# A drain of GpSimd between the row stores of the last two blocks of an attention and mixture-of-experts kernel

## The chip, the cores and the metric

The kernel runs on one NeuronCore of one Trainium2 chip. The metric is the device time of one execution in microseconds (us), taken as the median of several runs. A separate execution is recorded by the hardware profiler; its rows are quoted below.

## The reference

Four batches of 5056 tokens with 256 channels go through an attention over channels, and the result, 20224 rows of 256 values, through a mixture of eight experts of which each token takes the best one:

```python
qn = q / (norm(q, axis=1) + 1e-06); kn = k / (norm(k, axis=1) + 1e-06)
a = softmax(kn.transpose(0, 2, 1) @ qn / tau)
x = (v @ a).reshape(20224, 256)
logits = x @ w_gate + modality_bias[modality_id]
e_idx = argmax(logits); gate_w = softmax(logits)[e_idx]
for e in range(8):
    mask = e_idx == e
    out[mask] = gate_w[mask, None] * (relu(x[mask] @ w1[e]) @ w2[e])
```

## The kernel before, in words

All matrix products are made with numbers split into a high and a low part, three products for one. The kernel walks over 40 groups of 512 tokens. For each group it makes the rows of x, chooses each token's expert, and writes the rows to a place of that expert in a table in DRAM, `xs`. This takes four indirect DMAs of up to 128 rows each, issued by GpSimd (POOL in the profile).

The second half of the work is in blocks. A block is 512 rows of one expert: SyncE (SP) loads its rows and the expert's weights, TensorE (PE) multiplies by `w1` (`m1`, L642), ScalarE (ACT) and VectorE (DVE) apply the rectifier and split the result, PE multiplies by `w2` (`m2`, L658). `finish(t)` then scales a quarter of the block's result into the tile `yo` on ACT (L669), and `scatter` (L401) stores those 128 rows at their tokens' places in `out`, again with an indirect DMA of POOL. The rows on either side of such a DMA are found by a list of 128 indices in SBUF, and GpSimd builds the DMA's descriptors itself. There are 40 blocks in the usual case (`NB_MIN`), so POOL issues 160 such DMAs to `xs` and 160 to `out`.

After the last group only blocks are left. The pieces of a block run in program order; the stores of one block stand among the pieces of the next (`block_stream` puts the `last` pieces of the block before behind the first piece of the new one). The last block (slot 39) has its two halves finished one after the other: two stores, three more groups of products, two stores.

Behind the last block a value is read by all engines, and a branch on it decides whether further blocks are left over. In the usual case none are, the branch leads to the end, and there each engine's queue takes a few bookkeeping steps: POOL waits for the counts of its DMAs, executes one instruction that adjusts the semaphores of its DMAs (INC_SWDGE_SEM, L797), then a drain (L831); SP waits for the counts of all engines and DMAs; then all engines meet at a barrier, POOL clears the semaphores, and they meet again. This tail is not written in the kernel: it is what the framework puts behind every program. Lines of the kernel that the steps touch: `scatter` and its L401, `finish`, the loop `while chosen < NB_MIN or waiting`, and L797 and L831, which stand for the branch and for the program's end.

Of the kernel before, what the change touches and what calls it, by code (L numbers as in the profile page):

```python
# [34 lines left out]
def kernel(  # L35
# [13 lines left out]
    nc = tc.nc  # L49
# [17 lines left out]
    NB_MIN = -(-T // BLK)  # L67
# [81 lines left out]
    def pad_rows(r):  # L149
        ins = nc.sync.dma_start(  # L150
            xs[bass.ds(r, BLK), :].rearrange("(p t) c -> p t c", t=BLK // P),
            pad.unsqueeze(1).to_broadcast([P, BLK // P, XW]),
        )
        pads.append(ins.ins)
        tc.declare_no_dep(
            ins.ins, group="xr", reason="pads go past the last row of an expert, and before the blocks with them"
        )
# [242 lines left out]
    def scatter(dst, idx, rows, groups, add, bound, why):  # L400
        ins = nc.gpsimd.indirect_dma_start(  # L401
            out=dst, out_offset=bass.IndirectOffsetOnAxis(ap=idx, axis=0), in_=rows, in_offset=None,
            bounds_check=bound, oob_is_err=False,
        )
        for group in groups:
            tc.declare_no_dep(ins.ins, group=group, reason=why)
        for group in add:
            tc.add_to_no_dep_group(group, ins.ins)
        return ins.ins
# [130 lines left out]
        )  # L540


    def pick(g, slot, tail):
        nc.vector.tensor_copy(end9[:, 0:E], bases[g][0:1, :])
        sh = [1, E + 1]
        rem = p2.tile(sh, F32, tag="rem", name=f"rem_{slot}")
        nc.vector.tensor_tensor(rem, end9, nxt9, ALU.subtract)
        nc.vector.scalar_tensor_tensor(
            rem, rem, 1.0 if tail else float(BLK), prio9, ALU.is_ge, ALU.mult
        )  # L550
        m = p2.tile([1, 1], F32, tag="pm", name=f"pm_{slot}")
        nc.vector.tensor_reduce(m, rem, AX.X, ALU.max)  # L552
        nc.vector.tensor_scalar(rem, rem, m, None, ALU.is_equal)
        pr = p2.tile([1, 2, E + 1], F32, tag="pr", name=f"pr_{slot}")
        nc.vector.tensor_tensor(pr[:, 0, :], rem, nxt9, ALU.mult)
        nc.vector.tensor_tensor(pr[:, 1, :], rem, eid9, ALU.mult)
        pk = p2.tile([1, 2], F32, tag="pk", name=f"pk_{slot}")
        nc.vector.tensor_reduce(pk, pr, AX.X, ALU.add)
        pki = p4.tile([1, 2], I32, tag="pki", name=f"pki_{slot}")
        nc.vector.tensor_copy(pki, pk)  # L560
        nc.vector.tensor_tensor(rem, rem, inc9, ALU.mult)
        nc.vector.tensor_tensor(nxt9, nxt9, rem, ALU.add)
        return pki
# [5 lines left out]
    def block_pieces(g, slot, pki, tail):  # L569
# [18 lines left out]
        def load_w(hf):  # L588
            if hf == 0:
                st["e"] = nc.sync.value_load(pki[0:1, 1:2], min_val=0, max_val=E - 1)  # L590
            e = st["e"]
            a = p3.tile([P, CH, FH], F32, tag="w1r", name=f"w1r_{slot}_{hf}")
            c = p3.tile([P, JH, D], F32, tag="w2r", name=f"w2r_{slot}_{hf}")
            nc.sync.dma_start(
                a,
                w1[bass.ds(e, 1), :, hf * FH : (hf + 1) * FH].rearrange("o (h p) f -> p (o h) f", p=P),
            )
            nc.sync.dma_start(
                c,
                w2[bass.ds(e, 1), hf * FH : (hf + 1) * FH, :].rearrange("o (j p) c -> p (o j) c", p=P),  # L600
            )
            st["wr"][hf] = (a, c)
# [61 lines left out]
        def finish(t):  # L664
            if t == 0:
                st["yo"] = p2.tile([P, TT, D], F32, tag="yo", name=f"yo_{slot}")
            yo = st["yo"][:, t, :]
            xr = st["xr"].bitcast(F32)
            nc.scalar.activation(  # L669
                yo, st["y"][t // 2][:, t % 2, :], AF.Copy, scale=xr[:, t, D : D + 1]  # L670
            )
            scatter(
                out, st["xr"].bitcast(I32)[:, t, D + 1 : D + 2], yo, ["y"], ["y"], T - 1,
                "each token has a row of its own",
            )

        prep = [lambda: load_w(0), lambda: load_w(1), load_x]
        prep2 = [lambda: split_w(0), lambda: tr_x(0), lambda: tr_x(1), lambda: split_w(1)]
# [2 lines left out]
        for j in range(1, NJ):  # L681
# [5 lines left out]
            else:  # L687
                body.append(lambda j=j: m2(j - 1))
        last = [lambda: m2(NJ - 1)] + [lambda t=t: finish(t) for t in range(TT)]
        if slot == NB_MIN - 1:  # L690

            last = [lambda: m2(NJ - 1, range(0, 2)), lambda: finish(0), lambda: finish(1)]
            last += [lambda j=j: m2(j, range(2, 4)) for j in range(NJ - 3, NJ)]
            last += [lambda: finish(2), lambda: finish(3)]
# [3 lines left out]
    def run(pieces):  # L698
        for f in pieces:
            f()  # L700
# [10 lines left out]
    waiting = []  # L711
# [3 lines left out]
    def once(blk, what):  # L715
        key = (blk["slot"], what)
        if key not in done:
            done.add(key)
            run(blk[what])

    def block_stream(blk, nxt):

        once(blk, "load")
        once(blk, "prep")
        body = list(blk["body"])
        if nxt is not None:
            once(nxt, "load")
            done.add((nxt["slot"], "prep"))
            at = [len(body) * (i + 4) // 8 for i in range(len(nxt["prep"]))]
            for o, f in reversed(list(zip(at, nxt["prep"]))):  # L730
                body.insert(o, f)
        before = open_blk[0]["last"] if open_blk[0] is not None else []
        open_blk[0] = blk
        return [blk["first"]] + before + body
# [3 lines left out]
    for g in range(G):  # L738
        b, s = divmod(g, NS)
        streams = []  # L740
        for gg, blk in waiting:
            if gg <= g - LAG + 1:
                once(blk, "load")
        if len(waiting) > 0 and waiting[0][0] <= g - LAG:
            _, blk = waiting.pop(0)
            streams.append(block_stream(blk, waiting[0][1] if waiting and waiting[0][0] <= g - LAG + 1 else None))
        soft = list(softmax_pieces(b)) if s == 0 and b > 0 else []
        streams.append(soft + (va[g + 1][0] if g + 1 < G else []) + va[g][1])
        if b + 1 < B:
            streams.append(list(kq_pieces(b + 1, s)))  # L750
        _interleave(*streams)
        if waiting and waiting[0][0] <= g - LAG + 1:
            once(waiting[0][1], "load")
            once(waiting[0][1], "prep")
        if s == NS // 2 and b + 1 < B:
            setup_bias(b + 1)
        n = slots_by(g)
        while chosen < n:
            waiting.append((g, block_pieces(g, chosen, pick(g, chosen, False), False)))
            chosen += 1  # L760
# [7 lines left out]
    for e in range(E):  # L768
        r = nc.sync.value_load(endi[0:1, e : e + 1], min_val=0, max_val=E * CAP)
        pad_rows(r)  # L770
    while chosen < NB_MIN or waiting:
        while chosen < NB_MIN and len(waiting) < 2:
            blk = block_pieces(G - 1, chosen, pick(G - 1, chosen, True), True)
            once(blk, "load")
            waiting.append((G, blk))
            chosen += 1
        _, blk = waiting.pop(0)
        run(block_stream(blk, waiting[0][1] if waiting else None))
    run(open_blk[0]["last"])


# [5 lines left out]
    def left_over(slot, n):  # L787
        if n <= 0:
            return
        rem = p1.tile([1, E + 1], F32, tag="lrem", name=f"lrem_{slot}")  # L790
        nc.vector.tensor_tensor(rem, end9, nxt9, ALU.subtract)
        left = p1.tile([1, 1], F32, tag="left", name=f"left_{slot}")
        nc.vector.tensor_reduce(left, rem[:, 0:E], AX.X, ALU.max)
        lefti = p1.tile([1, 1], I32, tag="lefti", name=f"lefti_{slot}")
        nc.vector.tensor_scalar(lefti, left, 0.0, 1.0, ALU.max, ALU.min)
        lv = nc.values_load(lefti[0:1, 0:1], min_val=0, max_val=1)
        with tc.If(lv > 0):  # L797
            for i in range(min(n, 4)):
                blk = block_pieces(G - 1, slot + i, pick(G - 1, slot + i, True), True)
                run(blk["load"] + blk["prep"] + [blk["first"]] + blk["body"] + blk["last"])  # L800
            left_over(slot + 4, n - 4)
# [34 lines left out]
```

## Time and profile before

| what | us |
|---|---|
| median of 3 runs | 1270.14 |
| lowest and highest of them | 1269.83, 1273.26 |
| the profiled execution's own time | 1270.21 |
| its span, first to last instruction | 1268.1 |
| PE busy within the span | 1235.1 (97%) |
| POOL busy within the span | 348.6 (27%) |

The span lacks 2.1 us of the profiled execution's own time. "Busy" on the page counts an engine's work only. Instructions that only wait, set registers, branch or drain are left out of it, and so are the issues of DMAs on the queues. They appear in the view of one source line, under the name of the engine's queue (POOLq, SPq and so on), with the smallest, median and largest duration in ns and the start of the first and the last.

### The profile page before, as it was taken

Reading aid. Unit: us, or ns where it says so; the run is one execution under the profiler, and the core shown is the slowest. Engines: PE = TensorE matmul, PEld = TensorE weight load, DVE = VectorE, ACT = ScalarE, POOL = GpSimd, SP = SyncE. Lnnn points to the kernel's source line nnn. Section 1 sums busy time; section 2 is a strip of 40 time slices with the busy share of each in tenths; the row PEclk is TensorE's granted clock in tenths of the full one; section 3 lists DMA queues with packets and bytes.
Section 4 is the critical chain, followed back from the end, with each engine's and each line's share of the span. In section 5 each row is a group of like instructions: output and inputs, shape, how many; then the busy total and the mean of one; then the engine's idle time right before and its main releaser. Section 6 shows DMA issues by size and latency. Waiting matters only on the chain.

```text
span 1268.1 us, 24269 instructions
## 1 busy us (share of the span) xinstructions
PE 1235.1 (97%) x8368; PEld 1122.6 (89%) x8368; DVE 856.4 (68%) x2330; ACT 753.0 (59%) x1533; POOL 348.6 (27%) x348
## 2 busy tenths in 40 slices
PE   7998999999999999999999999999999999999994
PEld 6897988999999999999999999999999999999994
DVE  7898967867767767777777776565566655755541
ACT  6876756766666666766666665555555554555441
POOL 0036243232222223222232333222223332221121
PEclk9998999999999999999999999999999999999997
DMA  9759854555555555555555544345444444474300
GB/s 314 250 188 296 277 174 156 158 194 167 183 167 165 171 190 169 162 169 167 167 176 182 182 156 141 136 150 168 143 162 140 162 147 134 152 229 168 134 31 15
DMA packets 113124, 215.34 MB, mean 170 GB/s; under 512 B 16224, under 2 KB 61792, under 8 KB 112992
## 3 DMA queue, kind: packets, MB, share of 16 engines
q1 hardware_dynamic: 97632, 172.11, 43.6%
q0 software_dynamic: 15360, 41.60, 8.6%
q8 instruction: 67, 1.10, 0.4%
q14 instruction: 65, 0.53, 0.1%
HBM read 167.33 MB, written 46.60 MB: 169 GB/s over the span
## 4 chain that ended last, share of the span: by engine, by line
PE 80%; issue 3%; DVE 1%; DMA 1%; POOL 1%; ACT 0%; SPq 0%; POOLq 0%; DVEq 0%; ACTq 0%
PE hp L642 32%; PE y L658 32%; PE xp L469 8%; PE g L277 3%; PE vtp L453 2%; PE xtp L624 2%; PE g L281 2%; POOL out_dram L401 1%; DMA k<-in_k_dram 0%; DMA out_dram<-yo,xr 0%; PE ns L323 0%; PE gw L379 0%; DMA modi<-in_moe_modality_id_dram 0%; DVE hl L646 0%; PE atp L369 0%
## 5 line engine op out<-in xcount | busy, mean ns | idle before, releaser
L658 PE MATMUL y<-w2h,hh 128*128 128x256 f32 x1280 | 360.8, 282 | 0.0
L658 PE MATMUL y<-w2l,hh 128*128 128x256 f32 x1280 | 355.6, 278 | 0.0
L658 PE MATMUL y<-w2h,hl 128*128 128x256 f32 x1280 | 355.3, 278 | 0.0
L401 POOL DMA_INDIRECT xs<-x,pi x160 | 175.2, 1095 | 646.2 <-ACT w1h L613 467.5
L646 DVE SCALAR_TENSOR_TENSOR hl<-hp,hh 128x512 fp32r<-128x512 f32 x320 | 219.6, 686 | 132.5 <-ACT hh L645 131.8
L645 ACT ACTIVATE hh<-hp 128x512 fp32r<-128x512 f32 x320 | 191.9, 600 | 182.4 <-PE hp L642 182.3
L642 PE MATMUL hp<-xh,w1h 128*128 128x512 f32 x640 | 259.4, 406 | 0.2 <-ACT xh L629 0.2
L642 PE MATMUL hp<-xl,w1h 128*128 128x512 f32 x640 | 253.4, 396 | 1.2 <-DVE xl L630 1.2
L642 PE MATMUL hp<-xh,w1l 128*128 128x512 f32 x640 | 253.3, 396 | 0.0
L658 PEld LDWEIGHTS y<-w2h,hh 128*128 128x128 f32 x1280 | 240.3, 188 | 12.9 <-ACT hh L645 0.2
L658 PEld LDWEIGHTS y<-w2l,hh 128*128 128x128 f32 x1280 | 241.4, 189 | 11.5
L658 PEld LDWEIGHTS y<-w2h,hl 128*128 128x128 f32 x1280 | 239.5, 187 | 0.1
L401 POOL DMA_INDIRECT out_dram<-yo,xr x160 | 160.6, 1004 | 191.0 <-ACT yo L669 150.4
L614 DVE TENSOR_TENSOR w2l<-w2r,w2h 128x512 fp32r<-128x512 f32 x160 | 110.5, 691 | 70.5 <-ACT w2h L613 70.4
L642 PEld LDWEIGHTS hp<-xh,w1l 128*128 128x128 f32 x640 | 120.6, 189 | 28.7
L613 ACT CAST w2h<-w2r 128x512 fp32r<-128x512 f32 x160 | 100.2, 626 | 74.0 <-PE y L658 67.2
L614 DVE TENSOR_TENSOR w1l<-w1r,w1h 128x512 fp32r<-128x512 f32 x160 | 109.7, 686 | 49.3 <-ACT w1h L613 48.7
L642 PEld LDWEIGHTS hp<-xl,w1h 128*128 128x128 f32 x640 | 120.6, 189 | 16.1 <-DVE xl L630 1.7
L613 ACT CAST w1h<-w1r 128x512 fp32r<-128x512 f32 x160 | 100.9, 630 | 57.1 <-PE hp L642 56.7
L642 PEld LDWEIGHTS hp<-xh,w1h 128*128 128x128 f32 x640 | 120.2, 188 | 14.6 <-ACT xh L629 0.3
L277 PE MATMUL g<-qs,ks 128*128 128x512 f32 (+1 forms) x320 | 122.4, 405 | 6.5 <-DVE qs L252 5.7
L469 PE MATMUL xp<-ah,vh 128*128 128x264 f32 x320 | 96.3, 301 | 5.4 <-DVE pm L552 2.9
(151 smaller groups left out, 1852.0 us busy)
## 6 DMA issues: line engine op xcount, KB each, us to landing
w1r<-in_moe_w_dram SPq DMA_DIRECT2D x80, 512.0 KB, 3.5
w2r<-in_moe_w_dram SPq DMA_DIRECT2D x80, 512.0 KB, 3.5
xr<-xs SPq DMA_DIRECT2D x40, 516.0 KB, 4.8
v<-in_v_dram SPq DMA_DIRECT2D x36, 512.0 KB, 5.5
q<-in_q_dram SPq DMA_DIRECT2D x35, 512.0 KB, 9.2
k<-in_k_dram SPq DMA_DIRECT2D x35, 512.0 KB, 5.7
xs<-pad SPq DMA_DIRECT2D x9, 516.0 KB, 5.5
xs<-x,pi POOLq DMA_INDIRECT x160, 5.1
```

The lines of the kernel that those rows point to most:

```text
L277: nc.tensor.matmul(g, ks[:pp, t, m * P : (m + 1) * P], qs[:pp, t, :], start=first, stop=False, skip_group_check=True,)
L281: nc.tensor.matmul(g[:, 0:C], ks[:pp, t, C + m * P : C + (m + 1) * P], qs[:pp, t, 0:C], start=False, stop=last, skip_group_check=True,)
L401: ins = nc.gpsimd.indirect_dma_start(out=dst, out_offset=bass.IndirectOffsetOnAxis(ap=idx, axis=0), in_=rows, in_offset=None, bounds_check ...
L453: nc.tensor.matmul(tp[:, t * P : (t + 1) * P], st["v"][:, t, h * P : (h + 1) * P], ident, is_transpose=True, start=t == 0, stop=True, skip ...
L469: nc.tensor.matmul(xp[:, 0:DE], a[:, h, t * P : (t + 1) * P], w[:, h, :], start=i == 0, stop=i == len(seq) - 1,)
L613: nc.scalar.copy(hi, src)
L614: nc.vector.tensor_tensor(lo, src, hi.bitcast(F32), ALU.subtract)
L624: nc.tensor.matmul(tp[:, t * P : (t + 1) * P], st["xr"][:, t, h * P : (h + 1) * P], identr, is_transpose=True, start=t == 0, stop=True, sk ...
L642: nc.tensor.matmul(hp, w[:, h, fs], x[:, h, :], start=i == 0, stop=i == len(seq) - 1)
L645: nc.scalar.activation(hh, hp, AF.Relu)
L646: nc.vector.scalar_tensor_tensor(hl, hp, 0.0, hh.bitcast(F32), ALU.max, ALU.subtract)
L658: nc.tensor.matmul(y, a[:, tsl], w[:, j % 2, :], start=(j == 0 and i == 0 and t % 2 == 0), stop=(j == NJ - 1 and i == 2), skip_group_check ...
```

## The change

A drain instruction is put on POOL's queue behind the four stores of the last block but one (slot 38) and ahead of the four stores of the last block (slot 39). `stored` collects the former, `order` ties them to the drain and the drain to the latter; the ties are for the order on the one queue alone and carry no semaphore (`NoSync`). The drain is put into the last block's list of pieces four pieces before its end.

```diff
+    stored = []
+    drained = []
...
-            scatter(
+            ins = scatter(
                 out, st["xr"].bitcast(I32)[:, t, D + 1 : D + 2], yo, ["y"], ["y"], T - 1,
                 "each token has a row of its own",
             )
+            if slot == NB_MIN - 2:
+                stored.append(ins)
+            elif slot == NB_MIN - 1:
+                order(ins, drained)
...
+    def order(ins, others):
+        for other in others:
+            tc.add_manual_dep(
+                ins, other.name,
+                mybir.DependencyInfo(mybir.DependencyClass.NoSync, mybir.DependencyReason.DATA),
+                reason="order on the stores' queue",
+            )
+
+    def retire():
+        ins = nc.gpsimd.drain()
+        order(ins.ins, stored)
+        drained.append(ins.ins)
...
-        run(block_stream(blk, waiting[0][1] if waiting else None))
+        pieces = block_stream(blk, waiting[0][1] if waiting else None)
+        if not waiting:
+
+            pieces.insert(len(pieces) - 4, retire)
+        run(pieces)
```

In the built program this is one instruction more, on POOL's queue, between the fourth store of slot 38 and the first of slot 39. It waits for no semaphore and sets none. Every other instruction of every engine keeps its place and its waits.

## Rows read from the trace of the kernel before

**Rows 1.** The page: the span, and the busy time of PE and POOL.

```profile
span 1268.1 us, 24269 instructions
PE 1235.1 (97%) x8368; PEld 1122.6 (89%) x8368; DVE 856.4 (68%) x2330; ACT 753.0 (59%) x1533; POOL 348.6 (27%) x348
```

**Rows 2.** Windows over the last 38 us: stretch, length, busy time by engine, clock, DMA.

```profile
core 0: us, PE busy (x) PEld busy (x) DVE busy (x) ACT busy (x) POOL busy (x), PEclk, DMA share, GB/s
1230.00:1250.00 20.00, 20.00 (x132) 18.00 (x131) 5.46 (x8) 5.87 (x12) 3.49 (x5) 1.00 0.07 27
1250.00:1254.80 4.80, 0.72 (x7) 0.52 (x5) 0.00 (x0) 0.91 (x3) 3.87 (x4) 0.96 0.23 75
1254.80:1268.10 13.30, 0.00 (x0) 0.00 (x0) 0.00 (x0) 0.00 (x0) 0.00 (x0) 0.50 0.02 7
```

**Rows 3.** The chain that ended last, its end: start, length, what.

```profile
1249.98 3.44 DMA out_dram<-yo,xr
...
1253.81 0.97 POOL out_dram L401
```

**Rows 4.** POOL's timeline from 1225 us on: start, length, idle before and its end.

```profile
1229.58 0.97 POOL L401 DMA_INDIRECT out_dram<-yo,xr  x1 [18.28 <-ACT yo L669]
...
1233.41 0.97 POOL L401 DMA_INDIRECT out_dram<-yo,xr  x1 [0.31 <-issue]
1249.98 0.97 POOL L401 DMA_INDIRECT out_dram<-yo,xr  x1 [15.60 <-ACT yo L669]
1251.25 0.97 POOL L401 DMA_INDIRECT out_dram<-yo,xr  x1 [0.30 <-ACT yo L669]
1252.53 0.97 POOL L401 DMA_INDIRECT out_dram<-yo,xr  x1 [0.30 <-issue]
1253.81 0.97 POOL L401 DMA_INDIRECT out_dram<-yo,xr  x1 [0.30 <-issue]
```

**Rows 5.** L401 over the whole span, and, from 1229 us on, its DMAs' landing.

```profile
L401 POOL DMA_INDIRECT xs<-x,pi x160: 938/973/2542, 80.1 to 1091.6; - x160
L401 POOL DMA_INDIRECT out_dram<-yo,xr x160: 971/973/1533, 149.7 to 1253.8; - x160
...
DMA to landing us min/median/max: 2.3/2.4/2.4
```

**Rows 6.** The branch behind the last block, L797, on POOL from 1255 us on.

```profile
L797 POOLq EVENT_SEMAPHORE  x2: 43/43/43, 1255.3 to 1256.1; - x2
L797 POOLq INC_SWDGE_SEM  x1: 2306/2306/2306, 1256.2 to 1256.2; - x1
```

**Rows 7.** The program's end, L831, from 1258 to 1262 us: ns min/median/max, starts.

```profile
L831 SPq EVENT_SEMAPHORE  x12: 28/28/28, 1258.5 to 1259.2; - x12
L831 SPq DRAIN  x2: 7/10/13, 1259.2 to 1259.3; - x2
L831 POOLq DRAIN  x1: 8730/8730/8730, 1258.6 to 1258.6; - x1
```

**Rows 8.** L831 from 1262 us on, and the two later drains of POOL.

```profile
L831 POOLq EVENT_SEMAPHORE  x4: 17/17/17, 1267.3 to 1268.0; - x4
...
L831 POOLq EVENT_SEMAPHORE_RANGE_CLEAR  x1: 177/177/177, 1267.7 to 1267.7; - x1
...
L831 POOLq DRAIN  x2: 40/74/107, 1267.5 to 1267.9; - x2
```

**Rows 9.** The program's start, L818: the same two instructions of POOL.

```profile
L818 POOLq INC_SWDGE_SEM  x1: 31/31/31, 0.1 to 0.1; - x1
...
L818 POOLq DRAIN  x1: 188/188/188, 0.3 to 0.3; - x1
...
L818 POOL MEMSET const-uint8-127<- x1: 119/119/119, 0.3 to 0.3; 128x1 uint8 x1
```

**Rows 10.** Drains of the other engines at L831.

```profile
L831 DVEq DRAIN  x2: 10/14/17, 1251.3 to 1267.6; - x2
L831 PEldq DRAIN  x2: 8/8/8, 1252.9 to 1267.6; - x2
L831 ACTq DRAIN  x2: 8/8/8, 1254.2 to 1267.6; - x2
```

## The prediction

> **What bounds the kernel now.** I read the page first. PE is busy for 97% of the span [rows 1], so up to the last product nothing but PE's work sets the time, and an instruction on POOL, busy for 27%, can move the end only where PE has stopped. So the second view is the windows over the last stretch [rows 2]. The reader is to see three stages there. Until 1250.0 PE is busy without a gap. From 1250.0 to 1254.8 POOL issues the last stores. From 1254.8 to 1268.1, 13.3 us, no engine is busy at all, and the DMAs move almost nothing. The third view, the chain of waits, ends at 1253.81 + 0.97 = 1254.8 with the last store [rows 3]: it follows counted work and says nothing about those 13.3 us. They are 1.05% of the span, and they have to be read from the queues' own rows, by source line.
>
> Those rows give the tail step by step. The last store was issued at 1253.8 and lands 2.3 to 2.4 us later [rows 4, 5], which is when POOL's last wait for a count starts, 1256.1 [rows 6]. Then POOL executes INC_SWDGE_SEM from 1256.2 for 2.306 us, to 1258.5 [rows 6]. That instruction releases SP, whose twelve waits and two drains run from 1258.5 to 1259.3, 0.8 us [rows 7]. POOL itself goes into a drain at 1258.6 that lasts 8.730 us, to 1267.3 [rows 7]. Only then comes the barrier, from 1267.3 to 1268.1, 0.8 us [rows 8]. So the end waits for POOL's drain, and before it for INC_SWDGE_SEM: together 11.04 us.
>
> **What the two long instructions cost, and why.** The same pair stands at the program's start. There INC_SWDGE_SEM took 31 ns and POOL's drain 188 ns, which is no more than the memsets of some 119 ns beside it [rows 9]. Two later drains of POOL at the very end took 40 and 107 ns [rows 8]. What tells the long pair from the short ones is what stands between it and the drain before: 320 indirect DMAs ahead of the long pair [rows 5], none ahead of the short ones. All DMAs had landed when the long drain began, so it does not wait for data. The reading that fits is that POOL goes through something kept for each indirect DMA since the last drain: 8730 ns / 320 = 27 ns for each, if all 320 are still kept, or more for each if only the youngest are. INC_SWDGE_SEM, 2306 ns against 31, fits the same reading.
>
> What these rows show of drains can be weighed against a rule. The drains of VectorE, TensorE and ScalarE at the same line took 8 to 17 ns [rows 10], that of GpSimd 8730 ns [rows 7]. The Trainium skill (VectorE: DVE Perf Modes, The DRAIN you can't avoid) says that the drains which the runtime puts into every program are constant, about 12 ns, on all five engines. This case's trace agrees for the three and not for GpSimd. By that rule a drain here neither takes time nor clears anything, and the sum of the change would be zero; by the rows it is the sum below.
>
> **The change part by part.**
>
> - *Added: one drain behind the store of 1233.41.* That store ends at 1233.41 + 0.97 = 1234.4, and lands by 1233.41 + 2.4 = 1235.8 [rows 4, 5]. POOL is then idle until 1249.98, 15.6 us, waiting for `yo` of the last block [rows 4]. The drain meets 316 of the 320 DMAs. Its price lies between 0.04 us, the shortest drain of POOL [rows 8], and 8.73 us [rows 7]; if INC_SWDGE_SEM's work falls to it as well, 8.73 + 2.31 = 11.0 us. I take 316/320 of 8.73, 8.6 us, as it meets nearly the same DMAs. It ends between 1243.0 (from 1234.4) and 1244.4 (from the landing), and at 1246.8 with 11.0 us from the landing, so at least 3.2 us are left before the next store. The cost is nothing, and the cover is that idle time. Nothing else is queued on POOL; PE, ACT and DVE wait for no POOL instruction there, and SP has no load left that does. Without the cover each us would delay the last four stores and the end by the same.
> - *The last drain.* With four DMAs behind the new drain it has 4 x 27 ns = 0.11 us to go through, and some 0.1 to 0.2 us as the short drains [rows 8, 9]: 0.3 us instead of 8.73. But the 8.4 us do not all reach the end. The barrier then waits for SP, which is late next: its row ends at 1259.3, the drain would at 1258.9. So the barrier moves from 1267.3 to 1259.3: **8.0 us** off.
> - *INC_SWDGE_SEM.* Its price after the change lies between 0.03 us [rows 9] and 2.31 us [rows 6]. I take it near the lower end, because the four stores since the drain are its share of what made it long: 4 x 2306/320 = 29 ns, and 177 ns for adjusting semaphores, as the clearing of a range takes [rows 8]: 0.2 us. SP starts when it ends, so its 2.1 us come off SP's row and so off the end: **2.1 us**.
> - *The last four stores.* They may gain or lose: GpSimd's 0.3 us between stores [rows 4] may be bookkeeping for older DMAs, which would give back up to 3 x 0.3 = 0.9 us; a first store at the slowest price of the rows to `out`, 1.53 us instead of 0.97 [rows 5], costs 0.6 us. I take nothing, as the pace of 1.28 us is the same in all groups of stores.
>
> Sum: 1270.21 (the profiled execution) - 8.0 - 2.1 = **1260.1 us**. That execution lies 0.07 us above the median of the runs, so no correction is due. The gain is 0.8%; about 0.3%, 3.8 us, is what a measurement of this kernel can tell from no change.
>
> **The rivals.**
>
> 1. *Only the drain shrinks.* INC_SWDGE_SEM may be long because it adjusts semaphores that 320 DMAs have counted on, which a drain does not alter. For it: at the start there was nothing to adjust. Against it: the two get long and short together. Then 1270.2 - 8.0 = 1262.2 us.
> 2. *The drain is a price per use, not per DMA.* Any drain with an indirect DMA before it could cost 8.73 us, for instance a look at each queue or the loading of seldom used code; or a drain could clear nothing. Then the new one costs 8.7 us under cover, the last one 8.73 us again: 1270.2 us. The trace has only one long drain and can't exclude it. Against it speaks that INC_SWDGE_SEM, another instruction, is long too just there. The rule of 12 ns ends at the same time, 1270.2 us, by another way; as the trace denies it for GpSimd, it has little of this rival's chance. That the drain does nothing or stands elsewhere is excluded for its place: it stands between the stores in the built queue.
> 3. *The drain holds the last stores.* It sits at the head of POOL's queue, and the stores of the last block are behind it. It decides once it lasts beyond 1249.7, over 15.4 us from 1234.4, and every us over that is a us at the end. If in the middle it took the work of both long instructions twice, once for each kind of DMA, 2 x 11.0 = 22.1 us from 1234.4, and the last drain stayed, the stores would start 6.5 us late: 1276.7 us. For it: a fixed price is not excluded, and POOL does nothing ahead of time behind a drain. Against it: no instruction of POOL in the trace takes over 8.73 us.
>
> **How the numbers follow.** My forecast has 0.62, rival 1 has 0.22, rival 2 has 0.13 (0.01 of it for the rule of 12 ns), rival 3 has 0.03. So faster by over 0.3% has 0.84, within 0.3% 0.13, slower 0.03. The range goes from 1258.7, the forecast with INC_SWDGE_SEM at 0.03 us (1259.9), the 0.9 us of the stores and the 0.3 us by which the lowest run lies below the median, to 1264.0, rival 1 with a fifth of the long drain as a fixed part (1.7 us). It leaves out rivals 2 and 3, 0.16.
>
> **What the profile would show.** Right: a drain of POOL of 8 to 11 us that starts near 1234.4 and is over before 1249.7; the first store of the last block still near 1250.0; at the end INC_SWDGE_SEM well under 1 us and the drain under 0.5 us; SP's waits as the last step before the barrier, and about 3.3 us instead of 13.3 us between the last store's issue and the end. Rival 1 shows INC_SWDGE_SEM still at 2.3 us. The forecast is wrong if the last drain is still several us long, or if the first store of the last block starts after 1250.4.

## The result, and the profile after

| what | before | after the change |
|---|---|---|
| median of four runs on one chip, us | 1269.99 | 1260.04 |
| lowest and highest, us | 1269.44, 1273.26 | 1258.39, 1261.48 |
| ratio, with its 95% interval | | 0.991 [0.9897, 0.9923] |
| the profiled execution's own time, us | 1270.21 | 1258.93 |
| its span, us | 1268.1 | 1256.9 |
| last store's issue to the end of the span, us | 14.3 | 4.7 |

The page of the profile after, its span and its line of busy times, beside [rows 1]:

```profile
span 1256.9 us, 24270 instructions
PE 1233.9 (98%) x8368; PEld 1121.3 (89%) x8368; DVE 857.3 (68%) x2330; ACT 752.5 (60%) x1533; POOL 347.9 (28%) x348
```

One instruction more, and no engine's work differs by more than 1.3 us. The windows over the last stretch, beside [rows 2] (columns: stretch, length, busy time and count of PE, PEld, DVE, ACT and POOL, granted clock, DMA share, GB/s):

```profile
1230.00:1248.30 18.30, 18.30 (x121) 16.45 (x120) 4.74 (x7) 4.32 (x8) 2.12 (x3) 1.00 0.06 22
1248.30:1253.10 4.80, 0.77 (x7) 0.56 (x5) 0.00 (x0) 0.95 (x3) 3.86 (x4) 1.00 0.24 74
1253.10:1256.90 3.80, 0.00 (x0) 0.00 (x0) 0.00 (x0) 0.00 (x0) 0.04 (x1) 0.56 0.09 28
```

The three stages are the same three. The first two are as they were; the third, in which no engine works, has shrunk from 13.3 to 3.8 us. Now the new drain, L787, and POOL's timeline around it, beside [rows 4]:

```profile
L787 POOLq DRAIN  x1: 11650/11650/11650, 1229.5 to 1229.5; - x1
```

```profile
1231.75 0.97 POOL L401 DMA_INDIRECT out_dram<-yo,xr  x1 [0.30 <-issue]
1248.32 0.97 POOL L401 DMA_INDIRECT out_dram<-yo,xr  x1 [15.60 <-ACT yo L672]
...
1252.16 0.97 POOL L401 DMA_INDIRECT out_dram<-yo,xr  x1 [0.30 <-DMA out_dram<-yo,xr]
```

The drain's row starts at 1229.5, while two of the four stores ahead of it are still to be executed: the queue has taken it up, but it stands behind them. It ends at 1229.49 + 11.65 = 1241.14, which is 8.41 us behind the end of the fourth store (1231.75 + 0.97 = 1232.72). The next store starts at 1248.32, after 15.60 us of idle time that ACT's `yo` ends: to the hundredth the 15.60 us of before. The drain had 7.2 us to spare. The tail, at the branch (L821) and the program's end (L855), beside [rows 6, 7] (columns: ns min/median/max, first and last start):

```profile
L821 POOLq EVENT_SEMAPHORE  x2: 43/43/43, 1254.6 to 1254.9; - x2
L821 POOLq INC_SWDGE_SEM  x1: 264/264/264, 1255.0 to 1255.0; - x1
```

```profile
L855 SPq EVENT_SEMAPHORE  x12: 27/28/28, 1255.2 to 1255.9; - x12
L855 SPq DRAIN  x2: 7/10/13, 1256.0 to 1256.0; - x2
L855 POOLq DRAIN  x1: 386/386/386, 1255.3 to 1255.3; - x1
L855 POOLq EVENT_SEMAPHORE  x1: 17/17/17, 1256.1 to 1256.1; - x1
```

INC_SWDGE_SEM went from 2306 to 264 ns and the last drain from 8730 to 386 ns. The drain is over at 1255.7; SP's row ends at 1256.0, and the barrier's first wait on POOL starts at 1256.1. SP is now the last to arrive. Counted from the issue of the last store, the end comes 14.33 - 4.69 = 9.6 us sooner (1253.81 to 1268.14 before, 1252.16 to 1256.85 now).

The profiled executions differ by 11.28 us, 1.65 us more than that. The last store was issued at 1252.16 instead of 1253.81, and this lead is much older than the drain: the first store to `out` starts at 147.1 instead of 149.7, some 1080 us ahead of L787. The windows from 90 to 120 us, of the kernel before and then of the changed one:

```profile
90.00:120.00 30.00, 25.07 (x154) 21.06 (x154) 24.60 (x120) 19.48 (x45) 21.45 (x21) 0.91 0.87 277
```

```profile
90.00:120.00 30.00, 24.12 (x162) 20.06 (x162) 25.87 (x120) 19.91 (x48) 20.83 (x22) 1.00 0.86 275
```

In the execution profiled before, the granted clock was 0.91 there, a mean of stretches at either of its two levels, 1.2 and 2.4 GHz; in the one profiled after it was 1.00, the upper level throughout. PE's gaps were alike: it was busy for 25.07 and 24.12 of the 30 us. The clock is not all of it: 1.1 us of the lead stand already at the first store to `xs` (79.0 instead of 80.1), ahead of this stretch; it is 2.6 us at the first store to `out`, and from the fifth block on both run with the same steps, 1.7 us apart. It is not the change's doing as far as a run can tell: two of the changed kernel's four runs have a mean clock of 0.997 (1258.39 and 1258.93 us), two of 0.994 (1261.15 and 1261.48 us), and these are the same instructions. The medians, which include such differences on both sides, lie 9.95 us apart, near the tail's 9.6.

### The profile page after: what moved, and what is told of

It is laid out like the page before. It is cut to its first block, busy times and chain, and to the rows that moved or that the text cites. A ratio compares the mean times of both kernels' runs of the same rounds, so it can differ in the third digit from the quotient of the medians.

```text
span 1256.9 us, 24270 instructions
## 1 busy us (share of the span) xinstructions
PE 1233.9 (98%) x8368; PEld 1121.3 (89%) x8368; DVE 857.3 (68%) x2330; ACT 752.5 (60%) x1533; POOL 347.9 (28%) x348
## 4 chain that ended last, share of the span: by engine, by line
PE 82%; issue 3%; POOL 1%; DMA 0%; ACT 0%; DVE 0%; POOLq 0%; SPq 0%; DVEq 0%
PE hp L645 33%; PE y L661 32%; PE xp L469 8%; PE g L277 3%; PE vtp L453 2%; PE xtp L627 2%; PE g L281 2%; POOL out_dram L401 0%; PE ns L323 0%; DMA out_dram<-yo,xr 0%; PE gw L379 0%; DMA modi<-in_moe_modality_id_dram 0%; PE atp L369 0%; ACT yo L672 0%; PE rq L345 0%
## 5 line engine op out<-in xcount | busy, mean ns | idle before, releaser
L401 POOL DMA_INDIRECT xs<-x,pi x160 | 174.6, 1092 | 646.9 <-ACT w1h L616 469.5
L401 POOL DMA_INDIRECT out_dram<-yo,xr x160 | 160.5, 1003 | 190.8 <-ACT yo L672 150.2
```

The costliest lines, as they stand in the source:

```text
L401: ins = nc.gpsimd.indirect_dma_start(out=dst, out_offset=bass.IndirectOffsetOnAxis(ap=idx, axis=0), in_=rows, in_offset=None, bounds_check ...
```

## The experiments

**The theories.** A: every indirect DMA since the last drain is kept and costs the drain 27 ns and INC_SWDGE_SEM 7 ns (8730/320, 2306/320). B: only the youngest are kept, so each costs more. Behind these stands rival 2, a price per use. Twelve runs follow, in four sets; the kernels of a set share a chip and its runs of the kernel before, whose medians were 1308.00, 1321.13, 1322.84 and 1318.41 us. These chips lose time in the blocks in mid-program, not in the tail (the last experiments look into this); ratios are taken within a set.

Most kernels with more drains share one edit, in `scatter`; only the list CUTS differs, by the number of DMAs ahead of each drain:

```diff
+        if drained:
+            order(ins.ins, drained[-1:])
+        stored.append(ins.ins)
+        if len(stored) in CUTS:
+            d = nc.gpsimd.drain()
+            order(d.ins, stored)
+            drained.append(d.ins)
         return ins.ins
```

**again.** The changed kernel once more.

> The changed kernel once more, to see how far its runs lie apart and where. Theory: the change acts on the program's end alone. Then from the issue of the last store to the end it takes about 4.7 us as in the first profile of the change (1252.16 to 1256.9), against 14.3 us before, in every run; runs differ by 2 to 3 us through the stretch ahead of the last block, in step with the granted clock (0.994 to 0.997), and the kernel before shows such differences too. Median 1260 us, between 1258 and 1262. Rival: the drain also makes the stretch ahead of it shorter, by the 1.7 us by which the last block's first store came earlier (1248.3 instead of 1250.0). Then that store starts near 1248.3 in every profile of the change, at whatever clock, and the median is 1258.5 us.

Measured: 1297.05 against 1308.00 us, 0.9906 [0.9877, 0.9935]. The tail took 5.28 us (the last store landed in 3.4 us here), the new drain 11.66 us, INC_SWDGE_SEM 264 ns and the last drain 386 ns, as on the first chip. The gain and its place repeat. The 1260 us that were expected, and the rival's 1248.3, could not be tested, as this chip is slower as a whole.

**left160.** CUTS = (160,): one drain in the middle of the 320 DMAs, 160 behind it.

> One drain behind the 160th of the 320 indirect DMAs, so that 160 are left for the end. Theory A, everything since the last drain counts, 27 ns each: the last drain takes 160 x 27 ns = 4.4 us, INC_SWDGE_SEM about 1.2 us, and the time is 1264.6 us. Theory B, only a bounded number of the youngest is kept, about 70 ns each (386 ns for four, less the 107 ns of an empty drain, by 4), which makes (8730 - 107) / 70 = 123 of them: 160 fill that again, the last drain is 8.7 us and INC_SWDGE_SEM 2.3 us, and the time is 1270 us, as before. A drain in the middle of the program would then be worth nothing at all.

Measured: 0.9951 [0.9931, 0.9972], tail 9.01 us. The branch and the last drain:

```profile
L818 POOLq INC_SWDGE_SEM  x1: 1244/1244/1244, 1291.9 to 1291.9; - x1
L852 POOLq DRAIN  x1: 4382/4382/4382, 1293.2 to 1293.2; - x1
```

That is theory A's number for both, and B falls as it was put. Rival 2 falls too: a drain ahead does shorten the last one, and by a part.

**ladder_a, ladder_b.** CUTS = (8, 24, 56, 120, 248) leaves 72 DMAs for the last drain, CUTS = (112, 280) leaves 40.

> Five drains, with 8, 16, 32, 64 and 128 indirect DMAs ahead of each since the one before, and 72 left for the end: a scale of the price by number. Theory A (27 ns each, all kept): 0.3, 0.5, 1.0, 1.8 and 3.6 us, and 2.0 us for the last drain, 0.7 us for INC_SWDGE_SEM; time near 1262 us. Theory B (70 ns each, at most some 123 kept): 0.7, 1.2, 2.3, 4.6 and 8.7 us, and 5.1 us for the last drain, 1.4 us for INC_SWDGE_SEM; time near 1265.7 us. The drains in the middle also hold what is issued just ahead of them and lands, so their rows can be up to 4 us longer than these; the last one's row is free of that.

> Two drains, with 112 and 168 indirect DMAs ahead, and 40 left for the end. Theory A: 3.1 and 4.6 us in the middle, at the end 1.2 us and 0.5 us for INC_SWDGE_SEM; time near 1261 us. Theory B: 7.9 and 8.7 us, so the two nearly alike, at the end 2.9 us and 0.9 us for INC_SWDGE_SEM; time near 1263 us.

Measured: 0.9965 [0.9946, 0.9983] with a tail of 11.57 us, and 0.9934 [0.9912, 0.9956] with 7.82 us. The rows of ladder_a, then of ladder_b:

```profile
L818 POOLq INC_SWDGE_SEM  x1: 1626/1626/1626, 1292.7 to 1292.7; - x1
L852 POOLq DRAIN  x1: 5924/5924/5924, 1294.4 to 1294.4; - x1
```

```profile
L818 POOLq INC_SWDGE_SEM  x1: 984/984/984, 1297.5 to 1297.5; - x1
L852 POOLq DRAIN  x1: 3311/3311/3311, 1298.5 to 1298.5; - x1
```

72 DMAs cost more than 160 did: 5.9 us against 4.4. No price per DMA with all of them kept can do that, so A falls, and its hit with left160 was luck. The drains in mid-program, counted from the end of the DMA ahead of each, took 2.18, 2.75, 4.71, 7.25 and 2.80 us in ladder_a, with 8, 16, 32, 64 and 128 DMAs since the drain before, and in ladder_b 9.23 us with 112 and 5.04 us with 168. They rise up to 112 and fall behind it: B, by which 128 should cost as much as 320, falls as well.

**Theory C**, made from these rows: POOL keeps a list of its indirect DMAs. The last drain takes 61 ns and 81.6 ns for each that is kept (from 4, 40 and 72 DMAs: 386, 3311 and 5924 ns), INC_SWDGE_SEM 184 ns and 20 ns for each (264, 984, 1626 ns). A drain empties the list. When the list is full it sheds about 107 at once by itself; the 112 of ladder_b were still there in full (61 + 112 x 81.6 = 9200 ns, measured 9.23 us). The number kept, which the drain's row gives, then also gives INC_SWDGE_SEM's row. So what counts is not how many DMAs were issued but how many are left over:

| kernel | DMAs since the drain | kept | last drain, computed / measured, ns | INC_SWDGE_SEM, computed / measured, ns |
|---|---|---|---|---|
| before | 320 | 320 - 2 x 107 = 106 | 8711 / 8730 | 2304 / 2306 |
| left160 | 160 | 160 - 107 = 53 | 4386 / 4382 | 1244 / 1244 |
| ladder_a | 72 | 72 | 5936 / 5924 | 1624 / 1626 |
| ladder_b | 40 | 40 | 3325 / 3311 | 984 / 984 |
| the change | 4 | 4 | 387 / 386 | 264 / 264 |

These five rows made the theory; the next experiment and the later ones test it.

**extra12.** No drain at all; instead 12 indirect stores more, to spare DRAM tiles that nobody reads, so that the list should overflow a third time: 332 - 3 x 107 = 11 kept.

```diff
+            for t in range(TT if 20 <= g < 23 else 0):
+                spare = dram.tile([P, XW], ...)
+                nc.gpsimd.indirect_dma_start(
+                    out=spare[:, :], out_offset=bass.IndirectOffsetOnAxis(ap=lane, axis=0),
+                    in_=x[:, t, :], ...)
```

> No drain at all, but 12 indirect DMAs more, of four row stores each to spare DRAM tiles, in groups 20 to 22, where POOL has idle time (332 instead of 320). Theory C, made from the first four experiments: POOL keeps a list of its indirect DMAs; the last drain costs 61 ns and 81.6 ns for each one on it (386, 3311 and 5924 ns for 4, 40 and 72), INC_SWDGE_SEM 184 and 20 ns for each (264, 984, 1626 ns); a drain empties the list, and so does the list itself when it is full, which takes off about 107 at once (160 left read as 53, 320 as 106; 112 were still kept in full). Then 12 more run the list over once more before the end: 332 - 3 x 107 = 11 are left, the last drain takes 0.96 us and INC_SWDGE_SEM 0.40 us, and the kernel gains as much as the change, ratio about 0.992, with no drain in it. Rival theory D: the list shrinks by drains alone, and the reading for 160 has another cause. Then the last drain stays at 8.7 us or grows to 9.7 us, and the ratio is 1.000 to 1.001.

The rows of the tail:

```profile
L805 POOLq INC_SWDGE_SEM  x1: 404/404/404, 1328.2 to 1328.2; - x1
L839 POOLq DRAIN  x1: 972/972/972, 1328.6 to 1328.6; - x1
```

Computed 404 and 959 ns, measured 404 and 972, tail 4.80 us: with twelve DMAs **more** and no drain the tail is as short as with the change. That is theory C's sharpest hit. It also bounds the length: with 107 shed each time, the list is full at 113 to 118 DMAs, as 112 were still kept and 332 made it shed a third time. The time missed what was expected: 1.0053 [1.0026, 1.008]. The added DMAs were not covered: from one block's first rectifier on ACT to the next, two blocks just behind them took 41.17 and 37.42 us, where the kernel before on that chip (before_b) took 31.71 and 31.35, together 15.5 us (the next block gave 1.1 us back), more than the tail gives.

**uncovered.** CUTS = (318,): the drain stands between the second and the third store of the last block, where POOL does not sit idle.

> The drain of the change moved by two stores, between the second and the third store of the last block, where POOL has no idle time to cover it. Theory: its price is the same, about 8.4 us from the end of the second store, and now delays the last two stores by as much, so that the end's gain of some 10 us is spent: ratio 0.998 to 1.000. Rival: the price itself is hidden in the landing of the stores (2.3 to 3.4 us), and the ratio stays near 0.994.

Measured: 1.0009 [0.9985, 1.0033], a little above the 0.998 to 1.000 that were expected, by less than the interval; tail from the last store 4.23 us. The drain, the stores on either side and the last drain:

```profile
L427 POOLq DRAIN  x1: 10465/10465/10465, 1303.3 to 1303.3; - x1
```

```profile
1304.23 0.98 POOL L413 DMA_INDIRECT out_dram<-yo,xr  x1 [0.30 <-ACT yo L690]
1314.64 0.97 POOL L413 DMA_INDIRECT out_dram<-yo,xr  x1 [9.44 <-issue]
```

```profile
L852 POOLq DRAIN  x1: 223/223/223, 1318.6 to 1318.6; - x1
```

The drain ended 8.57 us behind the second store (kept: 318 - 214 = 104, computed 8548 ns), the third store waited 9.44 us, and the tail's gain was spent. So the change gains because the same work lies in POOL's idle 15.6 us.

**every8, before_b.** CUTS = range(8, 320, 8): 39 drains, which in the main stretch stand between a group's four stores to `xs` and the four stores to `out` that follow; and the kernel before, profiled on the same chip.

> A drain behind every eighth indirect DMA, 39 of them. Theory: each holds POOL for 2 to 3 us from the end of the DMA ahead of it, mostly for that DMA's landing, inside idle stretches of 15 to 20 us; with 8 left the last drain takes 0.7 us and INC_SWDGE_SEM 0.34 us, so the time is as with the one drain of the change, ratio 0.991 to 0.993. Rival: the rows of xs are issued later, the blocks' loads of them start later, and PE waits: each hold that reaches PE costs up to 2.5 us, all of them some 98 us, ratio up to 1.07.

> The kernel before, for its trace on the same chip as the three above. Theory: last drain 8.7 us and INC_SWDGE_SEM 2.3 us again, 14 to 15.5 us from the issue of the last store to the end; what differs from the first trace is the stretch ahead of the last block and the landing of the last store.

Measured: before_b 1329.10 us, last drain 8730 ns, INC_SWDGE_SEM 2306 ns, tail 15.06 us. every8: 1278.49 against 1321.13 us, 0.9675 [0.9638, 0.9711]; last drain 697 ns and INC_SWDGE_SEM 344 ns (8 kept: 714 and 344). Each of the 39 drains ends 0.36 to 0.38 us behind the landing of the DMA ahead of it, and that is 1.7 to 6.0 us behind that DMA's end. The DMA ahead of the last of them, the time from issue to landing of its block's four stores, and the drain:

```profile
1229.28 0.98 POOL L413 DMA_INDIRECT out_dram<-yo,xr  x1 [0.30 <-issue]
...
DMA to landing us min/median/max: 2.3/2.3/2.3
...
L427 POOLq DRAIN  x1: 4939/4939/4939, 1227.0 to 1227.0; - x1
```

The DMA landed at 1231.6 and the drain ended at 1231.9, where theory C alone gives 1231.0. So a drain also waits for what has not landed yet. This settles the drains of ladder_a and left160 that were longer than theory C gives: by the landings that their traces hold, they ended 0.38, 0.70, 0.90, 1.34, 2.22 and 2.65 us behind the last one, with 8, 16, 21, 32, 53 and 64 kept, which is 45 ns and 41 ns for each, half of theory C's price. The later of the two ends, theory C's from the end of the DMA ahead or this one from the landing, gives all drains in mid-program of all runs within 0.03 us, but for one of every8_late. No run was made to test it.

The tail is as expected, the time is not: some 32 us went that the tail never had (1321.13 - 1278.49, less 10.6 us of the tail). On this chip the blocks in the second half of the main stretch follow each other in 28.1 to 28.2 us in the kernel before, in 27.02 to 27.06 us with every8. On the chip of the result both kernels already do 27.02 to 27.06 us, as the kernel before here:

```profile
1007.27 1.30 POOL L401 DMA_INDIRECT xs<-x,pi  x1 [16.77 <-ACT w1h L613]
...
1034.32 1.30 POOL L401 DMA_INDIRECT xs<-x,pi  x1 [16.82 <-ACT w1h L613]
```

Two theories: L, a long list slows the DMAs that are issued; P, the pause between the two fours of stores helps, whatever makes it.

**every8_late, hold, every8_again.** CUTS = range(4, 320, 8) puts the drains of the main stretch behind the stores to `out`: the list stays short, the fours stay together. hold has no drain, and only waits with the first store to `out` until the four to `xs` have landed:

```diff
+        if dst is out and len(issued) < 2 * 4 * NB_MIN and issued and issued[-1][0] is not out:
+            after(ins.ins, [x for _, x in issued[-4:]])
+        issued.append((dst, ins.ins))
```

> A drain behind every eighth indirect DMA again, but moved by four: it stands behind the four stores to out, ahead of POOL's long idle time, and no longer between the four stores to xs and the four to out. The list is emptied as often; the pause between the two fours is gone. In the runs with 39 drains a block took 27.0 us in the second half of the main stretch, and 28.0 to 28.2 us in the other kernels on the same chip. Theory L, a long list itself slows the chip: steps of 27.0 us and a ratio of 0.966 to 0.970, as with the 39 drains before. Theory P, it is the pause between the fours that helps: steps near 28.1 us and a ratio of 0.990 to 0.993, the gain at the end alone. If this chip loses nothing in the main stretch, the ratio is 0.991 to 0.993 by both.

> No drain; the first store of each block waits until the four stores to xs ahead of it on POOL's queue have landed. This makes the pause of the 39 drains without emptying the list. Theory P: steps of 27.0 to 27.3 us in the second half of the main stretch, the end as before (drain 8.7 us), ratio 0.975 to 0.980. Theory L: steps near 28.1 us and a ratio of 0.998 to 1.003. If this chip loses nothing in the main stretch, the ratio is 1.000 by both.

> The kernel with 39 drains once more, on the same chip as the two above, to compare them with. On a chip that loses a us per block in the main stretch: ratio 0.962 to 0.972 as measured before; on one that does not, as the chip of the first two profiles: 0.991 to 0.993, the gain at the end alone.

Measured: every8_late 0.9946 [0.9925, 0.9967], hold 0.9741 [0.9714, 0.9767], every8_again 0.9665 [0.9638, 0.9692]. POOL's timeline of hold, one group and the start of the next:

```profile
1020.12 1.29 POOL L403 DMA_INDIRECT xs<-x,pi  x1 [13.58 <-DVE rem L558]
...
1024.27 0.97 POOL L403 DMA_INDIRECT xs<-x,pi  x1 [0.30 <-issue]
1028.01 0.97 POOL L403 DMA_INDIRECT out_dram<-yo,xr  x1 [2.77 <-DMA xs<-x,pi]
...
1047.19 1.29 POOL L403 DMA_INDIRECT xs<-x,pi  x1 [14.37 <-DVE rem L558]
```

A pause of 2.77 us, and the next group comes 27.07 us later. The same of before_b, without a pause, and of every8_late, whose list was as short as that of every8:

```profile
1028.12 1.30 POOL L401 DMA_INDIRECT xs<-x,pi  x1 [17.81 <-ACT w1h L613]
...
1032.28 0.97 POOL L401 DMA_INDIRECT xs<-x,pi  x1 [0.30 <-issue]
1033.56 0.97 POOL L401 DMA_INDIRECT out_dram<-yo,xr  x1 [0.30 <-issue]
...
1056.28 1.30 POOL L401 DMA_INDIRECT xs<-x,pi  x1 [17.92 <-ACT w1h L613]
```

```profile
1024.35 1.29 POOL L413 DMA_INDIRECT xs<-x,pi  x1 [17.87 <-ACT w1h L634]
...
1052.46 1.30 POOL L413 DMA_INDIRECT xs<-x,pi  x1 [17.88 <-DVE rem L574]
```

28.16 and 28.11 us. So L falls and P stands; what the pause does for PE is not shown. hold's tail stayed long, with the 8730 ns of before:

```profile
L836 POOLq DRAIN  x1: 8730/8730/8730, 1272.7 to 1272.7; - x1
```

every8_late had a last drain of 371 ns and a tail of 4.28 us; its ratio lies a little above what P made of it, as all that comes ahead of its tail took 3.6 us longer than in the kernel before (1315.67 - 4.28 against 1322.84 us less the 15.06 us of before_b); why was not tried.

**hold_drain.** The pause of hold and the one drain of the change.

> The two effects put together, one wait and one drain: the first store of each block waits for the landing of the four stores to xs ahead of it, as in the kernel with the hold alone, and the change's one drain stands ahead of the last block's stores. Theory: the two add up, as they act in different places. The steps of the main stretch are 27.0 us as with the hold, the end takes 4.3 to 5.3 us from the issue of the last store instead of 14 to 15, and the ratio is 0.974 - 0.0076 = 0.966 on a chip that loses a us per block, as with 39 drains; on one that does not, 0.991 to 0.993. Rival: the drain's 8.4 us and the hold get into each other's way and the ratio stays above 0.972.

Measured: 1277.77 against 1318.41 us, 0.9679 [0.9651, 0.9707]; tail 5.32 us, INC_SWDGE_SEM 264 ns, last drain 386 ns. The two effects add: hold alone gave 0.9741, and the change some 10 us of 1318, 0.992, of that. By the ratios this version beats the change alone, which had 0.9906 in its own set (again); the two did not run side by side. On the chip of the result, where the blocks lose nothing, it was not run.

## Why the prediction was right in its mechanism and wrong in its range

- *Faster by over 0.3%, with 0.84:* right, 0.991 [0.9897, 0.9923]. The median of the changed kernel, 1260.04 us, lies 0.1 us from the forecast's 1260.1. That is luck in part: the tail gave 9.6 us of the 10.1, and differences in the stretch ahead made up the rest.
- *The range, 1258.7 to 1264.0:* wrong at its low end. By the ratio the time is 0.991 x 1269.99 = 1258.6 us, 0.1 us below it, and one of the four runs, 1258.39 us, lies below it too. **The step that failed stands in "How the numbers follow":** the low end took "the 0.3 us by which the lowest run lies below the median" for all that executions may differ, from three runs of the kernel before. The runs showed more in its place: the four of the changed kernel lie from 1.65 us below their median to 1.44 us above it, two with a granted clock of 0.997 and two of 0.994, and the six of again lie 10.5 us apart. What happens in the 1250 us ahead of the edit is the larger unknown, and the range held next to nothing for it. The miss itself is small: the interval of the ratio runs from 1256.9 to 1260.2 us and takes in both the range's end and the forecast, and the ratio of the medians is 0.992. Above, the room up to 1264.0 was for rival 1, which did not come.
- *The added drain at nothing, 8.6 us under POOL's 15.6 us of idle time:* right. It took 8.41 us from the end of the store (its row, 11.65 us, starts ahead of two stores, which the prediction did not foresee); the next store did not move, so rival 3 falls. uncovered shows what it costs without its cover: the whole gain.
- *The last drain, 8.73 to 0.3 us, of which 8.0 us reach the end because SP is late next:* right. It took 0.386 us, and SP's row ended after it. The term came near by another way: it has 4 x 27 ns and 0.1 to 0.2 us, theory C 4 x 81.6 ns and 61 ns.
- *INC_SWDGE_SEM, 2.31 to 0.2 us:* right, 0.264 us; rival 1 falls by this row. Here too the working was near by luck: 4 x 7 ns and 177 ns in the prediction, 4 x 20 ns and 184 ns by theory C.
- *Nothing for the last four stores:* nearly. They kept the pace of 1.28 us; the last landed within 2.7 us instead of 2.4.
- *The sum of the tail:* 10.1 us predicted, 9.6 us measured in the profile. The later landing (0.42 us) makes most of the difference, and INC_SWDGE_SEM was 0.06 us longer than its term; the drain's 0.09 us more cost nothing, as SP was the last to arrive.
- *27 ns for each DMA:* wrong as a figure, though the sentence left the way out ("or more for each if only the youngest are"). It is 81.6 ns for each on the list and 106 of the 320 on it. It did no harm because four DMAs cost little at either price. For the drain in the middle "316/320 of 8.73" gave 8.6 us where the list, with 316 - 214 = 102 kept, gives 8.4: near, and by another way.
- *Two readings of the prediction that do not hold as they are put:* the 188 ns of the first drain are more than the 119 ns of the memset beside it, and "about 3.3 us instead of 13.3 us" counts from the end of the last store and not from its issue; so counted, 3.7 us were measured. Neither enters the sum.
- *The rule of 12 ns* (the Trainium skill, VectorE: DVE Perf Modes, The DRAIN you can't avoid): for GpSimd behind indirect DMAs the runs contradict it, from 223 ns with 2 kept to 8730 ns with 106.

What the runs don't settle: how the list's length at overflow and its shedding come about (107 and 112 are read off, not explained), and why a drain that had to wait for a landing then takes half the price for each DMA kept.

## What to carry to other kernels

Look at the tail behind the last counted instruction: the chain of waits ends before it, and only the rows by source line show it. If a GpSimd drain there is long and indirect DMAs of GpSimd ran before, put a drain where POOL is idle for as long as the drain lasts, the landing of the DMAs ahead of it included, and few DMAs follow; without such a gap it gained nothing here. And before a range is made for a small change, allow for what the long unchanged stretch varies by from one execution to the next.

## What the runs showed of the hardware that was not expected

- GpSimd's drain and INC_SWDGE_SEM are priced by a list that sheds about 107 DMAs by itself when full, and a drain waits for DMAs that have not landed. So the tail's length jumps with the number of DMAs: 72 kept cost 5.9 us, 160 issued 4.4 us, 320 issued 8.7 us, 332 issued 1.0 us.
- On the chips of the experiments, blocks whose eight indirect stores follow each other without a pause took about 1.1 us longer in the second half of the main stretch, on the chip of the result not. A wait of 2.8 us between the fours removes it: 0.9741 [0.9714, 0.9767] with hold. Comparing the starts of the matmuls of before_b and hold over six groups (945 to 1110 us), all of the excess, 6.7 us, falls 10 to 14 us behind a group's first store to `xs`, just behind the end of the eighth store (10.2 us). The granted clock was 1.00 in both. The view of PE's waits in before_b over that stretch names an engine for the smaller part of it:

```profile
PE hp L642 <- issue: 1.3, 4, 0.5
PE y L658 <- DVE hl L646: 1.2, 6, 0.2
```

That is 1.3 us in 4 waits of up to 0.5 us for "issue", which is no releaser that the profile shows, and 1.2 us in 6 waits for DVE's split of the block's values; hold has no such waits there. The other 4 us are in no wait of the view. What PE lacks there, and why one chip does not show it, stays open.
